# Block-sparse attention and a rational feed-forward: sampled key blocks copied by another engine, indices loaded four blocks at a time, factors in one instruction

## The chip, the cores and the metric

The kernel runs on one core of a Trainium2 chip. The metric is device time in microseconds, as the median of several runs. The engines are named as the profile names them: PE multiplies matrices (PEld loads its weights), DVE, ACT and POOL work on vectors, SP here only issues transfers (DMA). Each engine runs its instructions in the order in which the program was written for it.

## What is computed

Four batches of eight heads attend over 768 positions in 24 blocks of 32. A query block sees its neighbours, the first and the last block, and three sampled blocks; the first and last query block see all. The result, 3072 rows of 512, goes through a feed-forward whose activation is a quotient of polynomials.

```python
# attention: q, k, v are (4, 8, 768, 64)
scores = q @ k.T / sqrt(64)
mask = abs(blk_i - blk_j) <= 1
mask |= (blk_i == 0) | (blk_j == 0) | (blk_i == 23) | (blk_j == 23)
for qb in range(24):
    for kb in sampled_blocks[qb]:            # three per query block
        mask[qb*32:(qb+1)*32, kb*32:(kb+1)*32] = True
attn = softmax(where(mask, scores, -1e9))
x = (attn @ v) as (3072, 512)
# feed-forward: w_in is (512, 2048), w_out is (2048, 512)
h = x @ w_in
P = a[0] + a[1]*h + a[2]*h**2 + a[3]*h**3
Q = 1 + abs(b[0])*abs(h) + abs(b[1])*h**2
out = (P / (Q + 1e-6)) @ w_out
```

Weights and parameters `a`, `b` come as 64-bit floats, the indices as 64-bit integers; the kernel reads them as pairs of 32-bit words.

## The kernel before

**Tiles.** A key set (`kgs`, slices of the tile `kall`, and later `xkg`) holds eight blocks of keys: three neighbours, three sampled, the first and the last. A value set (`vgs`, shown as `vg`) holds the same eight blocks of values. The query block's scores against one key set are two tiles of 128 x 256 in `sp` (L903). DVE adds the bias of masked blocks and takes the maximum (`maxima`, L913), ACT takes the exponential (`exps`, L931), PE turns the result (L972), ACT evacuates it (`pT`, the helper's line L150), and PE multiplies it with the values (L1029, into `av`). Four query blocks together are weighted, turned and split into a high and a low half-precision part (`xh`, `xl`).

**Feed-forward.** Eight query blocks make a chunk of 256 rows; there are twelve chunks `c`. Each passes through eight units `u` of 256 columns of the hidden layer: 24 matmuls in (L1140 to L1142), the rational activation on ACT and DVE (L1147 to L1185), 12 matmuls out (L1196 to L1198). Each activation uses the factors in the tile `fc`, four per unit: the weight scale times 1, |b0|, a1 and a3. `factors` (L1114) writes them, for the first batch after each of four weight groups, for each later batch for all eight units at once.

**Weights.** The weights are decoded on the chip, one piece at a time: a transfer into `wl` (two buffers; L433 for `w_in`, L430 for `w_out`), a conversion (any of POOL, ACT, DVE, by the helper's line L150 or L154), three packing operations on DVE (L442, L445, L448), then scaling and splitting. This goes on while the first batch's attention and the first units run.

**The first batch's keys.** Its 24 key blocks stay in `kall`. Its sampled blocks are gathered from there: ACT copies three blocks of 128 x 256 in half precision into `kx` (two buffers, `kxs`; L856), each from an address in a register. Later batches gather keys by DMA from a scratch tensor `ks` (`kall<-ks`, L870 to L875). Values come by DMA in every batch (`vg`, L991 to L999): one transfer for the neighbours, two for the edges where they are not in place, three for the sampled blocks.

**The indices.** `ix` holds the clamped block numbers. `sampled_rows` (L795) loads the three of one query block into registers of the engine that needs them (TENSOR_LOAD): of SP for every query block and batch, of ACT for the first batch's copies. In a row of an order or a trace, ISA or FUSED_REGOPS beside a copy or a transfer is the arithmetic on such a register.

**The order.** Nothing is ordered by hand. Every piece of work is an `Op` with an engine (or several, by `among`), a price in nanoseconds, a priority and what it comes after. `issue` is a list scheduler: it simulates the engines with these prices and writes the program in the order in which its simulated engines take the pieces. A changed price or engine so changes the order on all engines. `fill` (L162) puts idle matmuls on PE where its simulation finds PE waiting in the first 80 us, to hold PE's clock.

Of the kernel before, what the change touches and what calls it, by code (L numbers as in the profile page):

```python
# [11 lines left out]
F32 = mybir.dt.float32  # L12
# [4 lines left out]
ALU = mybir.AluOpType  # L17
# [6 lines left out]
def kernel(  # L24
# [27 lines left out]
    nc = tc.nc  # L52
    B, H, S, D = q.shape
    DM, DFF = out.shape[1], w_out.shape[0]
    P = 128
    BLK = 32
    NB = S // BLK
    NR = sampled_blocks.shape[1]
# [15 lines left out]
    const = ctx.enter_context(tc.tile_pool(name="const", bufs=1))  # L74
# [21 lines left out]
    VE, SC, PO, TE, SY = "DVE", "Activation", "Pool", "PE", "SP"  # L96
# [193 lines left out]
    ix = const.tile([1, NB, 4], I32, name="ix")  # L290


    par = const.tile([P, 8], F32, name="par")
    absb = const.tile([P, 2], F32, name="absb")
    bias = const.tile([P, NB, NS], F32, name="bias")

    def load_small():
# [4 lines left out]
    def setup():  # L302
        nc.vector.tensor_scalar(out=ix[:, :, 0:NR], in0=samp[0:1].rearrange("p i (n w) -> p i n w", w=2)[:, :, :, 0],
                                scalar1=0, scalar2=NB - 1, op0=ALU.max, op1=ALU.min)
        nc.scalar.activation(out=absb, in_=par[:, 4:6], func=AF.Abs)

        sf = work[:, 2 * NR * NB:3 * NR * NB].rearrange("p (n i) -> p n i", n=NR)
        nc.vector.tensor_copy(out=sf, in_=samp.rearrange("p i (n w) -> p n i w", w=2)[:, :, :, 0])
        ii = work[:, 5 * NR * NB:5 * NR * NB + NB]
        nc.gpsimd.iota(ii, pattern=[[1, NB]], base=0, channel_multiplier=0, allow_small_or_imprecise_dtypes=True)  # L310
        dup = work[:, 3 * NR * NB:4 * NR * NB].rearrange("p (n i) -> p n i", n=NR)
        tmp = work[:, 4 * NR * NB:5 * NR * NB].rearrange("p (n i) -> p n i", n=NR)
        for r in range(NR):
            nc.vector.tensor_tensor(out=dup[:, r], in0=sf[:, r], in1=ii, op=ALU.subtract)
        nc.vector.tensor_tensor(out=dup, in0=dup, in1=dup, op=ALU.mult)
        nc.vector.tensor_scalar(out=dup, in0=dup, scalar1=1.0, scalar2=None, op0=ALU.is_le)
        for edge in (0.0, NB - 1.0):
            nc.vector.tensor_scalar(out=tmp, in0=sf, scalar1=edge, scalar2=None, op0=ALU.is_equal)
            nc.vector.tensor_tensor(out=dup, in0=dup, in1=tmp, op=ALU.max)
        for r in range(1, NR):  # L320
            for e in range(r):
                nc.vector.tensor_tensor(out=tmp[:, r], in0=sf[:, r], in1=sf[:, e], op=ALU.is_equal)
                nc.vector.tensor_tensor(out=dup[:, r], in0=dup[:, r], in1=tmp[:, r], op=ALU.max)
        nc.vector.memset(bias, 0.0)
        nc.vector.memset(bias[:, 1, 3 + NR:4 + NR], NEG)
        nc.vector.memset(bias[:, NB - 2, 4 + NR:5 + NR], NEG)
        for r in range(NR):
            nc.vector.tensor_scalar(out=bias[:, :, 3 + r], in0=dup[:, r], scalar1=NEG, scalar2=None, op0=ALU.mult)
# [195 lines left out]
    def block(j):  # L524
        return j + 1 if j < J else 0 if j == J else j
# [265 lines left out]

    def sampled_rows(x, eng=mybir.EngineType.SP):

        if (x, eng) not in rows_of:
            rows_of[x, eng] = nc.values_load_multi_w_load_instructions(  # L795
                ix[0:1, block(parts[x][1]), 0:NR], engines=[eng], min_val=0, max_val=NB - 1,
                skip_runtime_bounds_check_because="clamped when ix was written")[1]
        return rows_of[x, eng]

    def vrows(vg, kt, slot, n=1):  # L800
        return vg[slot * BLK:(slot + n) * BLK, kt].rearrange("p g a c -> p (g a c)")
# [21 lines left out]
    def attention(b, j, prio):  # L823
# [15 lines left out]
        for m, x in enumerate(xs):  # L839
            def one(m, x):  # L840
# [6 lines left out]
                if near and n > 1:  # L847
                    deps += [o for t in range(NCH) for o in k_evac[b, t]]
                    kslots = s_kall
                elif near:  # L850
                    s_kx = Slot(r_kx)

                    def copies():
                        rows = sampled_rows(x, mybir.EngineType.Activation)
                        for r in range(NR):
                            nc.scalar.copy(out=kxs[:, s_kx.buf, r].rearrange("p h r -> p (h r)"), in_=kall[:, bass.ds(rows[r], 1)].rearrange("p o h r -> p (o h r)"))  # L856

                    a = Op(SC, 1100, copies, [o_setup, chain["edges"]], p - 1, takes=[s_kx], uses=s_kall)
                    deps.append(a)
                    kslots = [s_kx] + s_kall  # L860
                else:
                    s_kg = Slot(r_kg)

                    def load():
                        kg, ks, = kgs[s_kg.buf], kv[b][0]
                        flat = kg.rearrange("p s h r -> p s (h r)")
                        if n > 1:
                            nc.sync.dma_start(out=flat, in_=ks[m * NS:(m + 1) * NS].rearrange("b p c -> p b c"))
                            return
                        nc.sync.dma_start(out=flat[:, 0:3], in_=ks[i - 1:i + 2].rearrange("b p c -> p b c"))  # L870
                        if h["new"]:
                            nc.sync.dma_start(out=flat[:, 3 + NR:], in_=ks[0:NB:NB - 1].rearrange("b p c -> p b c"))
                        rows = sampled_rows(x)
                        for r in range(NR):
                            nc.sync.dma_start(out=flat[:, 3 + r], in_=ks[bass.ds(rows[r], 1)].rearrange("o p c -> p (o c)"))  # L875

                    def price():
                        h["new"] = fresh("k", x, s_kg)
                        if n > 1:
                            return [(475, 524288)]  # L880
                        l = [(475, 196608)] + ([(475, 131072)] if h["new"] else [])
                        return l + [(860, 65536), (560, 65536), (560, 65536)]

                    a = Op(SY, price, load, [o_setup] + k_done[b], p - 1.95, takes=[s_kg], uses=[s_scr[b]], behind=chain.get("kg"))
                    chain["kg"] = a
                    deps.append(a)
                    kslots = [s_kg]
# [220 lines left out]
    def factors(b, u, n, after, prio):  # L1108

        def run():  # L1110
            if b not in fcs:
                fcs[b] = p2.tile([P, 4, NU], F32, name="fc")
            for j, coef in enumerate((1.0, absb[:, 0:1], par[:, 1:2], par[:, 3:4])):
                nc.vector.tensor_scalar(out=fcs[b][:, j, u:u + n], in0=wscale[:, u:u + n], scalar1=kv[b][3], scalar2=coef, op0=ALU.mult, op1=ALU.mult)  # L1114
        for x in range(u, u + n):
            o_fc[b, x] = None
        o = Op(VE, 700, run, after + [o_fc.get((b, 0))], prio)
        for x in range(u, u + n):
            o_fc[b, x] = o

# [246 lines left out]
```

## Time and profile before

| | |
|---|---|
| median of three timed runs | 882.49 us (882.07 to 882.88) |
| span of the profiled execution, first to last instruction | 879.5 us |
| its own time, taken as the median for want of another | 882.49 us, 3.0 around the span |
| busy PE / DVE / ACT / POOL | 824.0 / 730.5 / 676.5 / 111.5 us |
| granted clock of PE, mean | 0.985 |
| instructions on DVE / ACT / POOL | 1749 / 1449 / 115 |

The page also shows the span in 40 slices of 22 us; a digit is the busy share in tenths, 9 is 90% or more:

```
PE   8979686797899999899999999999999999999997
DVE  5658998999999888779878778878888787788886
ACT  6777897898678898987788768897898767588763
DMA  7797579868857955899556966899556966730000
```

Busy time on PE counts the filler too. Idle time of an engine that is not the bound costs nothing, so a stage is read by the engine that is full in it.

### The profile page before, as it was taken

How to read it: one execution, taken by the hardware profiler on the slowest of the kernel's cores; microseconds unless marked ns; L12 is line 12 of the kernel's file. 1: busy time of each engine (PE TensorE's matmuls, PEld its weight loads, DVE VectorE, ACT ScalarE, POOL GpSimd, SP SyncE). 2: the span in 40 equal slices, each digit the busy share in tenths (PEclk: the TensorE clock that was granted, in tenths of full speed). 3: DMA queues.
4: the chain of work that ended last, by engine and by line, in shares of the span. 5: the costliest groups of instructions: out<-in, count | busy, mean ns of one | idle time of the engine just before them, and what ended most of it. 6: DMA issues, size and time to landing. Idle time of an engine off the chain costs nothing.

```text
span 879.5 us, 27163 instructions
## 1 busy us (share of the span) xinstructions
PE 824.0 (94%) x10339; PEld 641.1 (73%) x10339; DVE 730.5 (83%) x1749; ACT 676.5 (77%) x1449; POOL 111.5 (13%) x115
## 2 busy tenths in 40 slices
PE   8979686797899999899999999999999999999997
PEld 4545465575678787778888787778788788788886
DVE  5658998999999888779878778888878787788886
ACT  6777897898678987788768887898767588767563
POOL 1123632616410000101000000100000000000000
PEclk9999899899999999999999999999999999999999
DMA  7797579868857955899556966899556966730000
GB/s 200 190 182 197 172 183 208 223 184 228 189 151 187 283 140 154 187 214 252 163 153 167 262 182 186 194 240 246 151 148 161 225 160 151 178 104 25 1 26 24
DMA packets 240209, 151.16 MB, mean 172 GB/s; under 512 B 16208, under 2 KB 222928, under 8 KB 240080
## 3 DMA queue, kind: packets, MB, share of 16 engines
q1 hardware_dynamic: 240080, 149.43, 68.6%
q8 instruction: 82, 1.34, 0.7%
q14 instruction: 47, 0.39, 0.2%
HBM read 132.07 MB, written 11.01 MB: 163 GB/s over the span
## 4 chain that ended last, share of the span: by engine, by line
PE 63%; DVE 13%; DMA 8%; SPq 7%; ACT 4%; issue 3%; POOL 1%; ACTq 0%; POOLq 0%; DVEq 0%
PE acc L1196 8%; PE ph L1140 8%; PE acc L1197 8%; PE acc L1198 8%; PE ph L1142 7%; PE ph L1141 7%; PE av L1029 5%; PE pt L972 4%; PE sp L903 4%; DMA vg<-in_v_dram 2%; SPq L999 2%; DMA wl<-in_moe_w_in_dram 2%; DVE pr L913 1%; DMA ldq<-in_q_dram 1%; DMA ld<-in_v_dram 1%
## 5 line engine op out<-in xcount | busy, mean ns | idle before, releaser
L1140 PE MATMUL ph<-xh,wi 128*128 128x256 f16 x768 | 211.7, 276 | 0.9 <-DVE tt L1157 0.9
L1141 PE MATMUL ph<-xl,wi 128*128 128x256 f16 x768 | 210.3, 274 | 0.0
L1142 PE MATMUL ph<-xh,wi 128*128 128x256 f16 x768 | 210.2, 274 | 0.0
L1196 PE MATMUL acc<-wo_h,gh 128*128 128x512 f32 x376 | 160.4, 427 | 0.2 <-ACT ld L150 0.2
L1198 PE MATMUL acc<-wo_h,gl 128*128 128x512 f32 x376 | 149.5, 398 | 3.8 <-DVE gl L1185 3.8
L1197 PE MATMUL acc<-wo_l,gh 128*128 128x512 f32 x376 | 149.1, 397 | 0.8 <-POOL wo_l L459 0.8
L1164 DVE SCALAR_TENSOR_TENSOR ab<-sq,absb,ab 128x512 f32<-128x512 f32 x96 | 73.3, 764 | 53.8 <-ACT ab L1161 53.8
L1147 ACT ACTIVATE sq<-ph,fc 128x512 f32<-128x512 f32 x96 | 65.7, 684 | 55.2 <-PE ph L1142 54.8
L1140 PEld LDWEIGHTS <-wi 128*128 128x128 f16 x768 | 75.4, 98 | 29.8 <-issue 16.2
L913 DVE CUSTOM_DVE_ANT_1 pr<-sp,bias 128x256 f32<-128x256 f32 x224 | 84.8, 418 | 8.3 <-PE sp L903 8.0
L931 ACT ACTIVATE pr<-pr,st,cqb 128x256 f32<-128x256 f32 x112 | 66.2, 594 | 31.0 <-DVE st L942 31.0
L1198 PEld LDWEIGHTS acc<-wo_h,gl 128*128 128x128 f32 x376 | 70.9, 189 | 21.6 <-DVE gl L1185 4.7
L1029 PE MATMUL av<-vg,pT 128*32 128x64 f32 x3584 | 74.9, 225 | 10.4 <-ACT pT L150 4.4
L1175 DVE SCALAR_TENSOR_TENSOR gh<-tt,par,rr 128x512 fp32r<-128x512 f32 x96 | 72.2, 752 | 14.4 <-PE acc L1197 12.9
L1196 PEld LDWEIGHTS acc<-wo_h,gh 128*128 128x128 f32 x376 | 71.3, 190 | 17.2 <-issue 2.1
L1029 PEld LDWEIGHTS av<-vg,pT 128*32 128x32 f32 x3584 | 56.9, 111 | 36.1 <-issue 14.6
L972 PE MATMUL pt<-ident,pr 128*128 128x128 f32 x448 | 74.6, 289 | 8.3 <-ACT pT L150 7.5
L1142 PEld LDWEIGHTS <-wi 128*128 128x128 f16 x768 | 75.5, 98 | 9.1
L972 PEld LDWEIGHTS pt<-ident,pr 128*128 128x128 f32 x448 | 68.0, 205 | 18.3 <-ACT pT L150 9.4
L1141 PEld LDWEIGHTS <-wi 128*128 128x128 f16 x768 | 75.6, 98 | 7.5
L1197 PEld LDWEIGHTS acc<-wo_l,gh 128*128 128x128 f32 x376 | 71.4, 190 | 13.0 <-POOL wo_l L459 1.7
L150 ACT ACTIVATE pT<-pt 128x512 f32<-128x512 f32 x112 | 66.3, 592 | 12.7 <-PE pt L972 12.0
(165 smaller groups left out, 1672.3 us busy)
## 6 DMA issues: line engine op xcount, KB each, us to landing
vg<-in_v_dram SPq DMA_DIRECT2D x312, 64.0 KB, 3.3
vg<-in_v_dram SPq DMA_DIRECT2D x88, 192.0 KB, 4.0
vg<-in_v_dram SPq DMA_DIRECT2D x24, 512.0 KB, 5.7
kall<-ks SPq DMA_DIRECT2D x49, 192.0 KB, 3.9
kall<-ks SPq DMA_DIRECT2D x147, 64.0 KB, 2.5
ld<-in_k_dram SPq DMA_DIRECT2D x36, 256.0 KB, 5.0
wl<-in_moe_w_in_dram SPq DMA_DIRECT2D x32, 256.0 KB, 4.4
wl<-in_moe_w_out_dram SPq DMA_DIRECT2D x16, 512.0 KB, 4.9
```

The costliest lines, as they stand in the source:

```text
L150: nc.scalar.activation(out=out, in_=in_, func=AF.Copy, scale=by)
L913: nc.vector.tensor_tensor_reduce(out=prs[x][:, g].rearrange("p (s r) -> p s r", r=BLK), in0=h["sp"][:, g].rearrange("p (s r) -> p s r", r= ...
L972: nc.tensor.transpose(pp[:, jj * P:(jj + 1) * P], cols, ident)
L1029: nc.tensor.matmul(av[rows, g], pT[:, 2 * g + kt, rows] if plain else pT[:, 2 * g + kt, pa_, rows], vf[:, g * HG + h4, kt * D:(kt + 1) * D ...
L1140: nc.tensor.matmul(o, wh, xh[:, :, cc], start=(cc == 0), stop=False)
L1141: nc.tensor.matmul(o, wh, xl[:, :, cc], start=False, stop=False)
L1142: nc.tensor.matmul(o, wl, xh[:, :, cc], start=False, stop=(cc == NCC - 1))
L1164: nc.vector.scalar_tensor_tensor(out=d["ab"], in0=d["sq"], scalar=absb[:, 1:2], in1=d["ab"], op0=ALU.mult, op1=ALU.add)
L1175: nc.vector.scalar_tensor_tensor(out=d["gh"], in0=d["tt"], scalar=par[:, 0:1], in1=d["rr"], op0=ALU.add, op1=ALU.mult)
L1196: nc.tensor.matmul(acc[:, t], ghs, wo_h[:, f], start=(new and e == 0), stop=False)
L1197: nc.tensor.matmul(acc[:, t], ghs, wo_l[:, f], start=False, stop=False)
L1198: nc.tensor.matmul(acc[:, t], gls, wo_h[:, f], start=False, stop=(last and e == 1))
```

## The change

Four edits, none of which changes what is computed:

- The copies of the first batch's sampled keys go from ACT to DVE, and their price for the scheduler from 1100 to 420 ns.
- `sampled_rows` loads the indices of four query blocks at once (three where an edge block is among them) and keeps the registers for the other three. SP's loads fall from 88 to 24; the copies' loads, 22 on ACT, become 6 on DVE.
- A weight group's four factors are one instruction over a tile `coef` of (1, |b0|, a1, a3), broadcast, in place of four; the price falls from 700 to 140.
- `setup` fills `coef` with four small DVE instructions.

```diff
+    coef = const.tile([P, 4], F32, name="coef")
...
         nc.scalar.activation(out=absb, in_=par[:, 4:6], func=AF.Abs)
+        nc.vector.memset(coef[:, 0:1], 1.0)
+        nc.vector.tensor_copy(out=coef[:, 1:2], in_=absb[:, 0:1])
+        nc.vector.tensor_copy(out=coef[:, 2:3], in_=par[:, 1:2])
+        nc.vector.tensor_copy(out=coef[:, 3:4], in_=par[:, 3:4])
...
-        if (x, eng) not in rows_of:
-            rows_of[x, eng] = nc.values_load_multi_w_load_instructions(
-                ix[0:1, block(parts[x][1]), 0:NR], engines=[eng], min_val=0, max_val=NB - 1,
+        b, j = parts[x][:2]
+        i = block(j)
+        if (b, i, eng) not in rows_of:
+            some = [n for n in (block(m) for m in range(j - j % 4, j - j % 4 + 4)) if n not in (0, NB - 1)]
+            values = nc.values_load_multi_w_load_instructions(
+                ix[0:1, some[0]:some[-1] + 1, 0:NR], engines=[eng], min_val=0, max_val=NB - 1,
                 skip_runtime_bounds_check_because="clamped when ix was written")[1]
-        return rows_of[x, eng]
+            for n, m in enumerate(some):
+                rows_of[b, m, eng] = values[n * NR:(n + 1) * NR]
+        return rows_of[b, i, eng]
...
-                        rows = sampled_rows(x, mybir.EngineType.Activation)
+                        rows = sampled_rows(x, mybir.EngineType.DVE)
                         for r in range(NR):
-                            nc.scalar.copy(out=kxs[:, s_kx.buf, r].rearrange("p h r -> p (h r)"), in_=kall[:, bass.ds(rows[r], 1)].rearrange("p o h r -> p (o h r)"))
+                            nc.vector.tensor_copy(out=kxs[:, s_kx.buf, r].rearrange("p h r -> p (h r)"), in_=kall[:, bass.ds(rows[r], 1)].rearrange("p o h r -> p (o h r)"))
-                    a = Op(SC, 1100, copies, [o_setup, chain["edges"]], p - 1, takes=[s_kx], uses=s_kall)
+                    a = Op(VE, 420, copies, [o_setup, chain["edges"]], p - 1, takes=[s_kx], uses=s_kall)
...
-            for j, coef in enumerate((1.0, absb[:, 0:1], par[:, 1:2], par[:, 3:4])):
-                nc.vector.tensor_scalar(out=fcs[b][:, j, u:u + n], in0=wscale[:, u:u + n], scalar1=kv[b][3], scalar2=coef, op0=ALU.mult, op1=ALU.mult)
+            nc.vector.scalar_tensor_tensor(out=fcs[b][:, :, u:u + n], in0=wscale[:, u:u + n].rearrange("p (o n) -> p o n", o=1).broadcast_to([P, 4, n]), scalar=kv[b][3],
+                                           in1=coef.rearrange("p (j o) -> p j o", o=1).broadcast_to([P, 4, n]), op0=ALU.mult, op1=ALU.mult)
-        o = Op(VE, 700, run, after + [o_fc.get((b, 0))], prio)
+        o = Op(VE, 140, run, after + [o_fc.get((b, 0))], prio)
```

The new prices change the scheduler's order on every engine. The number of fill matmuls falls from 201 to 182, and of the work that several engines may take, POOL has five operations fewer, DVE two fewer and ACT seven more.

The first place is DVE at the start of the first batch's attention, just ahead of the first maxima. `cq` and `hlq` belong to the queries, `kx` is the copies' target, `pr` the scores with their bias. Before:

```order
L741 SCALAR_TENSOR_TENSOR cq_451<-scq_425,sc0_236 128x1
L744 TENSOR_SCALAR cq_451<-cq_451 128x1
L747 TENSOR_SCALAR cq_451<-cq_451 128x1
L386 SCALAR_TENSOR_TENSOR hlq_453<-ldq_321,scq_425,hlq_453 128x8x64
L913 ISA pr_536,st_535<-sp_502,bias_102 128x256
L913 ISA st_535 128x1
```

After:

```order
L746 SCALAR_TENSOR_TENSOR cq_460<-scq_441,sc0_259 128x1
L803 TENSOR_LOAD ix_99
L866 ISA
L866 COPY kx_113<-kall_109 128x256
L866 ISA
L866 COPY kx_113<-kall_109 128x256
L866 ISA
L866 COPY kx_113<-kall_109 128x256
L391 SCALAR_TENSOR_TENSOR hlq_462<-ldq_344,scq_441,hlq_462 128x8x64
L749 TENSOR_SCALAR cq_460<-cq_460 128x1
```

A load of indices and three copies now stand on DVE between the queries' factors; two more sets of three follow before the first maxima. In all 39 copies and four loads stand ahead of the first unit's arithmetic, 27 copies and two loads behind.

The second place is SP between the third and the fourth piece of `w_in` (`wl`), with the value sets (`vg0` to `vg2`) between. Before:

```order
L433 DMA wl_734<-in_moe_w_in_dram 64x1024 x2
L993 DMA vg0_109<-in_v_dram 48x8x128
L795 TENSOR_LOAD ix_99
L999 ISA
L999 DMA vg0_109<-in_v_dram 16x8x128
L999 ISA
L999 DMA vg0_109<-in_v_dram 16x8x128
L999 ISA
L999 DMA vg0_109<-in_v_dram 16x8x128
L433 DMA wl_877<-in_moe_w_in_dram 64x1024 x2
```

After, from the last of the value sets that stand there:

```order
L1003 DMA vg1_111<-in_v_dram 48x8x128
L1009 ISA
L1009 DMA vg1_111<-in_v_dram 16x8x128
L1009 ISA
L1009 DMA vg1_111<-in_v_dram 16x8x128
L1009 ISA
L1009 DMA vg1_111<-in_v_dram 16x8x128
L438 DMA wl_1234<-in_moe_w_in_dram 64x1024 x2
L438 DMA wl_1255<-in_moe_w_in_dram 64x1024 x2
```

One value set stood between the third and the fourth piece, five stand there now, and the fifth piece follows at once; four of the five sets have no index load of their own.

## The prediction

> **What bounds the kernel now.** I read the table of stretches first, then the page's busy totals, then who waits for whom, then the chain. The columns of a stretch are its bounds, its length, and busy time (with the count) of PE, PEld, DVE, ACT and POOL, then granted clock, DMA share and GB/s.
>
> ```profile
> span 879.5 us, 27163 instructions
> 27.00:80.00 53.00, 46.02 (x719) 27.67 (x718) 32.99 (x102) 40.70 (x109) 13.33 (x16) 0.97 0.93 195
> 80.00:254.00 174.00, 140.57 (x2072) 105.29 (x2071) 170.12 (x409) 146.01 (x330) 74.63 (x64) 0.94 0.79 195
> 254.00:340.00 86.00, 86.00 (x1068) 69.41 (x1069) 77.25 (x204) 72.81 (x163) 2.85 (x3) 1.00 0.73 189
> 340.00:400.00 60.00, 56.09 (x758) 45.08 (x757) 45.10 (x115) 48.23 (x103) 3.54 (x4) 1.00 0.86 202
> 400.00:880.00 480.00, 471.43 (x5593) 382.11 (x5590) 388.71 (x863) 351.03 (x712) 12.85 (x16) 1.00 0.61 153
> L162 PE MATMUL acc<-ident 128*128 128x512 f16 x201 | 53.4, 402 | 1.7 <-DVE ident L93 1.7
> ```
>
> The filler alone (L162), a stretch before 100 us and the one behind, first PE and then PEld:
>
> ```profile
> 80.00:100.00 20.00, 6.41 (x25) 2.02 (x24) 0.89 0.49 148
> 100.00:120.00 20.00, 0.00 (x0) 0.00 (x0) 0.93 0.81 218
> ```
>
> Three stages. From 27 to 80 us no compute engine is full, DMA is (0.93), and much of what PE does is filler (53.4 us, none of it after 100 us). From 80 to 254 us DVE is busy 170.12 of 174 us and PE is not: DVE bounds it. From 254 us on PE is the bound: it stands idle 60 - 56.09 = 3.9 us from 340 to 400, and 8.6 us after. The span is therefore settled by how soon DVE gets through its work up to about 254 us, and by PE's few gaps behind. A microsecond taken off DVE between 80 and 254 us is a microsecond of the end; off ACT there (146 of 174) it is not.
>
> **The copies.** ACT's copies by stretch (its busy time), then their group, the price of an index load, and three rows that say how a load is hidden:
>
> ```profile
> 27.00:80.00 53.00, 9.77 (x30) 0.97 0.93 195
> 80.00:254.00 174.00, 12.05 (x36) 0.94 0.79 195
> L856 ACT COPY kx<-kall x66: 377/402/430, 26.9 to 176.4; 128x256 f16 x66
> L795 SPq TENSOR_LOAD <-ix x88: 664/675/1877, 13.9 to 754.9; - x88
> L795 ACTq TENSOR_LOAD <-ix x22: 696/703/932, 25.3 to 173.6; - x22
> 28.24 1.02 ACT L856 COPY kx<-kall 128x256 f16 x3 [0.36 <-issue]
> 35.04 1.00 ACT L856 COPY kx<-kall 128x256 f16 x3
> L442 DVE TENSOR_SCALAR dw<-dw x16: 411/416/1431, 85.7 to 240.6; 128x512 int32<-128x512 int32 x16
> L152 DVE COPY kall<-ph x6: 705/712/731, 18.1 to 26.1; 128x512 f16<-128x512 f16 x6
> ```
>
> Removed from ACT: 9.8 us before 80 us and 12.1 us after. The second part is off the path. The first sits in the attention's chain, but in a stretch whose DMA is full, so I book it at nothing; what is late next there is the transfer of values and weights.
>
> Added to DVE: 66 copies. No DVE copy of 128x256 f16 from SBUF is in the trace. Below: L442 moves four times the bytes in 0.41 us, a quarter is 0.10. Above: half of L152 (twice the elements, from PSUM), 0.36. I take 0.17, nearer to L442, which like the copy reads one operand in SBUF. In the new order 39 copies stand on DVE ahead of the first weight unit's arithmetic, which before began at 78.0 us (row below): 39 x 0.17 = 6.6 us, into the 53 - 32.99 = 20.0 us in which DVE idles from 27 to 80 us. Cost 0 while that cover lasts. What DVE waits for there is mainly the weights, not what the copies delay:
>
> ```profile
> DVE wi L442 <- POOL wi L154: 7.8, 4, 3.4
> DVE ab L1164 <- ACT ab L1161: 2.8, 1, 2.8
> 78.00 0.75 DVE L1164 SCALAR_TENSOR_TENSOR ab<-sq,absb,ab 128x512 f32<-128x512 f32 x1 [2.85 <-ACT ab L1161]
> ```
>
> The other 27 copies fall in the full stage: 27 x 0.17 = +4.6 us (2.7 to 9.7). They may also meet POOL, busy 74.63 of 174 us with operations of 74.63 / 64 = 1.2 us: nine groups of three, 0.43 of them met for half an operation, +2.3. Against this the new order gives POOL five operations fewer (conversions of weights go to ACT), 5.8 us; where two in five of them made DVE wait, that is as much. I let the two cancel.
>
> **The index loads.** 110 loads of three values become 30 of up to twelve, 24 on SP and 6 on DVE. A load stands ahead of each group of three copies: at 28.24 it left ACT idle for 0.36 of its 0.70 us, at 35.04 for none, since ACT had work queued. I take 0.35 us for one on DVE, four of them ahead of the first unit (in the idle 20 us, 0) and two in the full stage: +0.7. Below 0; above, if time goes by the values loaded, 4 x 0.70 = 2.8 us each.
>
> On SP 64 loads fewer are 64 x 0.675 = 43 us of its time, spread over all batches. Where SP sets the pace that is worth something. The chain of waits from 345 to 360 us runs through SP, where two of the longer pieces are index loads, and PE waits just then:
>
> ```profile
> 349.82 0.68 SPq L795
> 357.27 0.68 SPq L795
> 353.12 0.65 PE L1029 MATMUL av<-vg,pT 128*32 128x64 f32 x32 [0.90 <-DMA vg<-in_v_dram]
> 357.17 0.32 PE L343 MATMUL sp<-ident,mxq 128*128 128x128 f32 x1 [1.54 <-ACT scrap L392]
> ```
>
> Three of four loads gone at about 7 us apart over some 30 us is 2.0 us, and the two waits above are 2.4. A new order may open a gap elsewhere, 0.5: -1.5 us (-6 to +3).
>
> **The factors.** DVE's busy time in the three groups of four L1114 after 80 us; below, what one costs beside POOL and what it costs alone:
>
> ```profile
> 88.00:91.20 3.20, 3.11 (x4) 1.00 0.72 204
> 158.50:162.50 4.00, 3.98 (x4) 1.00 1.12 329
> 204.30:207.00 2.70, 2.62 (x4) 1.00 0.86 212
> 158.52 1.13 DVE L1114 TENSOR_SCALAR fc<-wscale,sc 128x2 f32<-128x2 f32 x1
> 159.56 1.20 DVE L1114 TENSOR_SCALAR fc<-wscale,sc,absb 128x2 f32<-128x2 f32 x1
> 158.46 3.39 POOL L506 TENSOR_TENSOR wi<-dw,wi 128x512 f16<-128x512 f32 x3
> 633.15 0.22 DVE L1114 TENSOR_SCALAR fc<-wscale,sc 128x8 f32<-128x8 f32 x1
> 633.28 0.28 DVE L1114 TENSOR_SCALAR fc<-wscale,sc,absb 128x8 f32<-128x8 f32 x1
> ```
>
> An instruction on two values takes 1.1 to 1.2 us while POOL works, 0.2 to 0.3 when it does not: it pays for waiting, once each. Twelve of them cost 9.7 us of the full stage. Three in their place, each 0.2 to 1.2, taken at 0.5: 1.5. Gain -8.2. The first group lies where DVE idles, and the later batches' groups lie under PE: 0. The four small instructions that fill coef stand ahead of a wait of DVE that ends on ACT at 12.34 us and was 3.98 us long:
>
> ```profile
> 12.34 0.16 DVE L613 TENSOR_REDUCE mx<-mx 128x1 f32<-128x6 f32 x1 [3.98 <-ACT scrap L392]
> ```
>
> Cost 0.
>
> **Sum.** Full stage +4.6 + 0.7 - 8.2 = -2.9; early stage 0; late stage -1.5: -4.4 on a span of 879.5, so 875.1. The timed median, 882.49, stands 3.0 above this span; I add it: 878.1 us. In the early stage bounds are -5 to +6: on the good side ACT's 9.8 us shorten attention by half, on the bad side the next rivals.
>
> **A rule against it.** All loads in the trace have three values, so 0.675 us may be a fixed price or 0.225 a value; no row can tell.
>
> The Trainium skill, "Runtime: NRT & Kernel Launch", section on instruction fetch mechanics, puts a register load at about 200 ns per register, in bulk too (for loads from HBM); by that page twelve values would be an estimated 2.4 us, DVE's six loads 14.4 us, and SP's saving nearly nothing. "DMA: Bandwidth & Descriptors", section on latency and other measured facts, gives instead a floor of about 600 ns for such a load, which would bear out the gain. The trace's 0.675 agrees with both, so I leave it a rival.
>
> **Rivals.** *A load goes by its values (slower).* Mechanism: DVE's in-order queue stands behind a load; maxima and weight packing wait, and PE for those. At 2.8 us, of which 0.7 is covered by queued work as at 35.04, each costs 2.1: two in the full stage 4.2 instead of 0.7, four early 8.4, half of it into the idle time, 4.2; SP's 1.5 is not gained. 878.1 + 3.5 + 4.2 + 1.5 = 887.3. It decides where two full and four half loads eat the 4.4 and their 0.7, from about 2.0 us a load. For it: the fit above. Against: loads were seen hidden.
>
> *The weights fall behind the values (no change).* SP issues the fourth piece of w_in one set of values after the third; in the new order five sets stand between. A set is
>
> ```profile
> vg<-in_v_dram SPq DMA_DIRECT2D x312, 64.0 KB, 3.3
> vg<-in_v_dram SPq DMA_DIRECT2D x88, 192.0 KB, 4.0
> ```
>
> 192 + 3 x 64 = 384 KB, four more are 1.5 MB, at 195 GB/s 7.9 us. If the first unit starts that much later and attention done in the meantime returns only half, +4: 882.1. Against: five sets stand there because attention runs earlier.
>
> *Attention gains too (more).* DVE's idle 20 us shrinks by 6 as scores stop waiting for ACT: 872.
>
> **How the numbers follow.** Forecast 0.42, more gain 0.12, no change 0.22, slower 0.24. What this kernel's measurement can tell from no change is 0.2%, 1.8 us. Faster 0.54, same 0.22, slower 0.24. The range leaves out the best and worst tenths: 870 to 889; the forecast's own is 874 to 880.7.
>
> **What would show it.** By the changed file's lines: right are L866 at 0.1 to 0.25 us on DVE, L803 near 0.7 us on both queues, L1123 below 0.6 us; DVE still full from 80 to 250 us; PE without gaps some 3 us sooner; less than 3.9 us idle about 340 to 400. Wrong: L803 of 2 us or more with DVE idle behind it, copies of 0.35 us or more, or the first L1150 over 5 us later with no attention ahead to show for it; then the sum is off by its place.

## The result, and the profile after

The changed kernel is slower: 890.56 us in the median of six runs (888.86 to 895.68) against 881.92 of the kernel before beside it, a ratio of 1.0109 with a 95% interval of 1.0085 to 1.0133. The forecast was 878.1 us. The profiled execution of after has a span of 888.2 us.

The stretches of after, with the columns as before:

```profile
span 888.2 us, 27041 instructions
27.00:80.00 53.00, 44.98 (x796) 26.00 (x795) 33.62 (x153) 31.03 (x80) 9.25 (x13) 0.94 0.84 186
80.00:254.00 174.00, 137.49 (x1866) 103.85 (x1866) 160.36 (x394) 133.43 (x286) 72.09 (x62) 0.87 0.75 192
254.00:340.00 86.00, 84.84 (x1029) 68.30 (x1027) 73.86 (x178) 71.91 (x160) 2.92 (x3) 0.98 0.76 207
340.00:400.00 60.00, 58.68 (x764) 47.15 (x762) 51.67 (x139) 49.09 (x103) 6.33 (x7) 1.00 0.70 188
400.00:880.00 480.00, 476.45 (x5722) 386.33 (x5720) 392.91 (x870) 356.21 (x724) 13.10 (x15) 1.00 0.58 152
400.00:860.00 460.00, 456.45 (x5603) 369.90 (x5601) 375.12 (x844) 346.61 (x709) 13.10 (x15) 1.00 0.60 159
```

The last stretch of before, up to 860 us too:

```profile
400.00:860.00 460.00, 456.45 (x5517) 370.32 (x5515) 376.15 (x845) 345.62 (x704) 12.85 (x16) 1.00 0.63 159
```

The loss is in the first 254 us. DVE, which had 3.9 us to spare between 80 and 254 us, now has 13.6 (174 - 160.36), although it was given more to do. PE's granted clock there falls from 0.94 to 0.87. Behind it PE is a little fuller than before only from 340 to 400 us, where it is idle for 1.3 us (3.9 before). From 400 to 860 us it is idle for 3.55 us in both kernels. The rows to 880 us can't be compared: before ends at 879.5 us, so its thinly filled last microseconds all lie in the row, while after runs on to 888.2.

Followed through the trace, the output matmuls of unit 24 (counted from 0, in the order of execution) begin at 346.0 us before and at 358.9 after, 12.9 us later; those of unit 88 at 841.8 and 850.6, 8.8 later. So some 13 us are lost early and 4 are gained back by unit 88.

The three parts by their groups, of after. (Two of DVE's six loads and eight of SP's 24 carry nine values, because an edge block is among their four; the others carry twelve.) A group's row has the shortest, median and longest duration in ns, then its first and last start:

```profile
L803 SPq TENSOR_LOAD <-ix x24: 1908/2528/2724, 13.9 to 751.0; - x24
L803 DVEq TENSOR_LOAD <-ix x6: 2115/2828/3067, 27.4 to 168.6; - x6
L866 DVEq FUSED_REGOPS  x66: 57/57/65, 30.5 to 181.3; - x66
L866 DVE COPY kx<-kall x66: 173/220/1302, 30.6 to 183.3; 128x256 f16 x66
L1123 DVE SCALAR_TENSOR_TENSOR fc<-wscale,sc,coef x7: 247/391/1112, 75.5 to 642.1; 128x8 f32<-128x8 f32 x4, 128x32 f32<-128x32 f32 x3
```

Copies and factors have medians of 0.22 and 0.39 us, near the forecast's 0.17 and 0.5; some of each take over 1 us. A load of twelve values takes 2.53 us on SP and 2.83 on DVE; one of three took 0.675 and, on ACT, 0.70. It goes by its values.

For whom DVE waits from 27 to 80 us, in after (us in total, times, longest):

```profile
DVE kx L866 <- issue: 7.0, 3, 3.1
DVE xn L1073 <- PE av L1039: 5.1, 1, 5.1
DVE kx L866 <- PE sp L913: 4.0, 3, 2.6
DVE xl L1097 <- ACT xh L150: 1.6, 1, 1.6
```

The first row is the load itself: no engine releases the copy, and a load of 2.79 us on DVE, begun at 71.56, ends just ahead of the copy at 74.53. The second is new in kind: the weighing of query blocks 4 to 7 (`xn`) waits for value matmuls, and it stands in DVE's row ahead of the packing of the fourth piece of `w_in`. The steps to the first unit, in the trace of before and then of after:

```profile
52.37 0.69 DVE L445 SCALAR_TENSOR_TENSOR wi<-wl,wi 128x512 int32<-128x512 int32 x1
62.57 0.22 DVE L489 COPY wscale<-scw 128x1 f32<-128x1 f32 x2
62.58 2.06 POOL L154 TENSOR_SCALAR dw<-wi,scw 128x512 f32<-128x512 f32 x3 [10.71 <-DVE scw L360]
65.30 0.69 DVE L1063 TENSOR_TENSOR xn<-av,sm 128x512 f32<-128x512 f32 x1 [1.14 <-PE av L1029]
73.88 0.27 PE L1140 MATMUL ph<-xh,wi 128*128 128x256 f16 x1
```

```profile
61.71 0.69 DVE L1073 TENSOR_TENSOR xn<-av,sm 128x512 f32<-128x512 f32 x1 [5.06 <-PE av L1039]
64.31 0.66 POOL L154 TENSOR_SCALAR wi<-wl 128x512 f32<-128x512 f32 x1 [14.54 <-DMA wl<-in_moe_w_in_dram]
65.46 0.69 DVE L450 SCALAR_TENSOR_TENSOR wi<-wl,wi 128x512 int32<-128x512 int32 x1
74.53 0.50 DVE L866 COPY kx<-kall 128x256 f16 x3 [2.83 <-issue]
75.19 2.03 POOL L154 TENSOR_SCALAR dw<-wi,scw 128x512 f32<-128x512 f32 x3 [10.22 <-DVE scw L365]
84.32 0.28 PE L1150 MATMUL ph<-xh,wi 128*128 128x256 f16 x1
```

Before, the fourth piece is packed at 52 us, the scale is ready at 62.6 and the weighing comes after that. After, the weighing comes first and waits, the fourth piece comes from memory only at 64.3, and a load of twelve values (2.83 us) stands in the middle of the scale's small steps. POOL gets the scale 12.6 us later, the first unit begins 10.4 us later.

### The profile page after: what moved, and what is told of

Same layout as the page of the kernel before. It is cut to its first block, busy times and chain, and to the rows that moved or that the text cites. A ratio compares the mean times of both kernels' runs of the same rounds, so it can differ in the third digit from the quotient of the medians.

```text
span 888.2 us, 27041 instructions
## 1 busy us (share of the span) xinstructions
PE 828.8 (93%) x10320; PEld 645.5 (73%) x10320; DVE 731.1 (82%) x1796; ACT 659.8 (74%) x1390; POOL 108.0 (12%) x110
## 4 chain that ended last, share of the span: by engine, by line
PE 61%; DVE 16%; ACT 7%; SPq 6%; DMA 5%; issue 4%; DVEq 1%; POOL 0%; POOLq 0%; ACTq 0%
PE ph L1150 8%; PE acc L1206 8%; PE acc L1208 7%; PE acc L1207 7%; PE ph L1151 7%; PE ph L1152 7%; PE av L1039 5%; PE sp L913 4%; PE pt L982 4%; SPq L1009 2%; ACT pr L941 2%; DVE pr L923 2%; DMA wl<-in_moe_w_in_dram 1%; DVE gh L1185 1%; DMA ldq<-in_q_dram 1%
## 5 line engine op out<-in xcount | busy, mean ns | idle before, releaser
L1150 PE MATMUL ph<-xh,wi 128*128 128x256 f16 x768 | 214.5, 279 | 2.0 <-DVE tt L1167 2.0
L1151 PE MATMUL ph<-xl,wi 128*128 128x256 f16 x768 | 212.9, 277 | 0.0
L1152 PE MATMUL ph<-xh,wi 128*128 128x256 f16 x768 | 212.8, 277 | 0.0
L1174 DVE SCALAR_TENSOR_TENSOR ab<-sq,absb,ab 128x512 f32<-128x512 f32 x96 | 72.5, 755 | 58.5 <-ACT ab L1171 58.4
L1150 PEld LDWEIGHTS <-wi 128*128 128x128 f16 x768 | 76.6, 100 | 30.2 <-issue 16.6
L982 PE MATMUL pt<-ident,pr 128*128 128x128 f32 x448 | 76.9, 292 | 12.2 <-ACT pT L150 7.3
L1185 DVE SCALAR_TENSOR_TENSOR gh<-tt,par,rr 128x512 fp32r<-128x512 f32 x96 | 74.7, 778 | 16.0 <-PE acc L1207 12.6
L1151 PEld LDWEIGHTS <-wi 128*128 128x128 f16 x768 | 76.6, 100 | 10.5 <-issue 2.0
L1152 PEld LDWEIGHTS <-wi 128*128 128x128 f16 x768 | 76.5, 100 | 10.2
L1207 PEld LDWEIGHTS acc<-wo_l,gh 128*128 128x128 f32 x376 | 71.7, 191 | 12.6 <-POOL wo_l L464 0.8
L941 ACT ACTIVATE pr<-pr,st,cq 128x256 f32<-128x256 f32 x112 | 66.2, 597 | 19.0 <-DVE st L952 19.0
```

The lines of the kernel that those rows point to most:

```text
L941: nc.scalar.activation(out=prs[x][:, g], in_=prs[x][:, g], func=AF.Exp, scale=Q["first"]["c"], bias=st[:, 6 + g:7 + g], accum_out=total if ...
L982: nc.tensor.transpose(pp[:, jj * P:(jj + 1) * P], cols, ident)
L1150: nc.tensor.matmul(o, wh, xh[:, :, cc], start=(cc == 0), stop=False)
L1151: nc.tensor.matmul(o, wh, xl[:, :, cc], start=False, stop=False)
L1152: nc.tensor.matmul(o, wl, xh[:, :, cc], start=False, stop=(cc == NCC - 1))
L1174: nc.vector.scalar_tensor_tensor(out=d["ab"], in0=d["sq"], scalar=absb[:, 1:2], in1=d["ab"], op0=ALU.mult, op1=ALU.add)
```

## The experiments

"The planner" is the list scheduler. Each kernel was timed in five rounds against the kernel before on the same chip; the median is followed by the ratio to it with its 95% interval.

### One part after another, in two orders

**Factors alone.** The kernel before, with the one instruction for a group's factors. The price of 700 is kept, so the planner writes the same order; the four small instructions that fill `coef` come with it.

```diff
-            for j, coef in enumerate((1.0, absb[:, 0:1], par[:, 1:2], par[:, 3:4])):
-                nc.vector.tensor_scalar(out=fcs[b][:, j, u:u + n], ...)
+            nc.vector.scalar_tensor_tensor(out=fcs[b][:, :, u:u + n], ...)
         o = Op(VE, 700, run, ...)
```

> The kernel before with the factors in one instruction alone, at the old price, so that the order stays. My prediction's term (each of the twelve instructions beside POOL paid a wait of its own): 8 us less, 873 to 876. Rival (the wait for POOL moves to the next instruction that needs it): 2 to 3 us less, 879 to 881.

875.75 us, 0.9926 (0.9898 to 0.9954): -6.5 us. The term of the factors, -8.2, is nearly there, and the rival's 2 to 3 us lie outside the interval. The seven instructions take 3.7 us in all, 525 ns each:

```profile
L1118 DVE SCALAR_TENSOR_TENSOR fc<-wscale,sc,coef 128x8 f32<-128x8 f32 (+1 forms) x7 | 3.7, 525 | 0.0
```

**Copies in the old order.** The kernel before, the copies and their loads of three values issued on DVE, at the places where ACT's stood in the plan:

```diff
-                        rows = sampled_rows(x, mybir.EngineType.Activation)
+                        rows = sampled_rows(x, mybir.EngineType.DVE)
-                            nc.scalar.copy(out=kxs[...], ...)
+                            nc.vector.tensor_copy(out=kxs[...], ...)
                     a = Op(SC, 1100, copies, ...)
```

> The kernel before, its order kept (the scheduler still plans the copies on ACT at 1100 ns), with the copies issued on DVE and loads of three. Theory A: copies cost little, 27 to 36 of them at 0.17 us in DVE's full stage, +3 to +6 us, ACT's relief early takes half back: 882 to 886. Theory B (only the new order is bad): no change or a gain, 878 to 882.

887.47 us, 1.0057 (1.0037 to 1.0078): +5.0 us. Its copies between 80 and 254 us (busy time of DVE, count, clock, DMA share, GB/s):

```profile
80.00:254.00 174.00, 7.39 (x36) 0.89 0.79 188
```

DVE is as full from 80 to 254 us as before (170.17 us busy, 170.12 before) although copies are 7.39 us of it, so some 7 us of its other work come later. The time lies above both expectations. The loss is of the size of what the copies take of a full DVE; what ACT's relief gives back was not measured apart.

**Factors and copies in the old order.** Both of these edits.

> The old order with both: copies issued on DVE (loads of three) and factors in one instruction. Against the changed kernel with loads of three (888.0) only the order differs. If the two edits add (+0.57% and -0.74%): 880 to 882. Theory B then puts 6 to 7 us on the new order. Theory C: 886 to 888, the same as in the new order.

883.15 us, 1.0014 (0.9996 to 1.0032). Against the factors alone the copies cost 0.88%, 7.8 us. The gain of one part is spent by the other. In both of these kernels the copies stand where the order planned them for ACT; the third order below has them at places planned for DVE.

**Grouped loads in the old order.** The kernel before with `sampled_rows` of after; six loads of up to twelve values on ACT, 24 on SP.

> The kernel before with the grouped loads alone (24 of twelve values on SP, 6 on ACT), order kept. Theory A (by value): SP's sum of loads stays near 60 us, ACT waits about 2 us in each of its six, early ones on the path: +2 to +6 us, 884 to 888, and no gain from SP late. Rival (a fixed price, the long loads of the changed kernel come from elsewhere): -2 us, 879 to 880.

882.40 us, 0.9981 (0.9958 to 1.0004): nothing that the measurement can tell. The rows say why:

```profile
L798 SPq TENSOR_LOAD <-ix x24: 1903/2526/2716, 13.8 to 743.7; - x24
L798 ACTq TENSOR_LOAD <-ix x6: 1981/2653/2828, 25.2 to 141.8; - x6
```

16 loads of twelve values and 8 of nine are 16 x 2.53 + 8 x 1.91 = 55.8 us on SP, and 88 x 0.675 = 59.4 before: there was next to nothing to save.

**After with loads of three.** The kernel after with `sampled_rows` of before; order, copies and factors as in after.

> The changed kernel with one edit taken back: indices are loaded three at a time again (88 loads on SP, 22 on DVE), order and copies stay. Theory A (a load goes by its values: 2.83 us for twelve, DVE idle 11.1 us before the copies): loads fall back to about 0.68 us, DVE's idle time before the copies to under 3 us, the kernel wins 6 to 9 us back, to 880 to 884. Theory B (the new order itself is late: the first unit starts at 84 instead of 74 us, PE's granted clock sinks to 0.87 between 80 and 254 us): idle time goes, but time stays at 886 to 890.

887.96 us, 1.0055 (1.0034 to 1.0077). So twelve values a load cost 0.54% on DVE. And this kernel does the same work as the one with factors and copies in the old order (1.0014), apart from 182 filler matmuls in place of 201 and some conversions that went from POOL and DVE to ACT: the new order costs 0.41%, with intervals that only just don't overlap. The profiled execution of this run is its longest, 6.6 us above the median, and some 2.6 us late before any of this begins (its first matmuls into `ph` start at 18.3 us, in after at 15.7). Its times within the trace are to be read with that in mind.

**Loads of six**, after with two blocks to a load.

> The kernel after with its order, and loads of six values (two blocks) in place of twelve. A load goes by its values: 1.4 us each on VectorE and 1.35 us on SP (3 values took 0.75 and 0.67, 12 took 2.83 and 2.53), 44 of them on SP, and the ratio between that with loads of three (1.0055) and that with twelve (1.0109), near 1.007. Rival (the load's floor counts, values cost little, and twelve are slow for another reason): below 1.0 us each, ratio 1.005 or less.

884.14 us, 1.0036 (1.0018 to 1.0055). The durations follow the values, the ratio doesn't lie between its neighbours as expected. Twelve values are worse than three or six; between these two the intervals overlap.

```profile
L803 SPq TENSOR_LOAD <-ix x48: 664/1298/2692, 13.8 to 757.4; - x48
L803 DVEq TENSOR_LOAD <-ix x12: 743/1429/1814, 27.3 to 176.3; - x12
```

**The new order with the copies on ACT.** After with loads of three, the copies issued on ACT at DVE's places.

> The changed kernel's order kept (the scheduler still plans the copies on DVE at 420 ns), but the copies are issued on ACT, with loads of three; factors in one instruction. Its counterpart in the old order is the run with factors alone (875.8). Theory B (the new order itself is late): 882 to 886, so 6 to 10 us over its counterpart, although DVE carries no copies. Theory C (the copies' 0.16 to 0.2 us each on a full DVE explain the loss, order costs nothing): 875 to 879.

888.85 us, 1.0070 (1.0046 to 1.0095), the same as with the copies on DVE (1.0055). Taking the copies off DVE gains nothing here, although DVE is busy for only 154.19 us from 80 to 254. That doesn't show that the copies cost nothing on DVE: they now stand in ACT's row at places planned for DVE, and in the third order (below) that alone loses time.

### Which order, and why

**A third order.** After with loads of three; the planner is told a price of 700 for the copies, and nothing else is changed.

```diff
-                    a = Op(VE, 420, copies, ...)
+                    a = Op(VE, 700, copies, ...)
```

> The changed kernel with loads of three, the copies priced at 700 instead of 420 ns for the scheduler: a third order of the same instructions, in which three sets of values instead of five stand between the weights' third and fourth piece. Theory B in the form that the weights fall behind the values: the first unit starts some 5 us earlier than at 84 to 86 us and the time falls to 881 to 885. If it is not the weights, time stays within 2 us of 888.

876.16 us, 0.9950 (0.9928 to 0.9972), against 1.0055 for the same work at a price of 420 (DVE, ACT and POOL have as many instructions in both, PE has four filler matmuls more). The order alone is worth 1.05%, 9.3 us. Only one set of values, not three as expected, stands on SP between the third and the fourth piece, as in the kernel before; the fourth is issued at 49.2 us, in after at 58.5. The first unit begins at 68.6 us. Waits of DVE from 27 to 80 us:

```profile
DVE kx L861 <- issue: 5.1, 8, 1.0
DVE xl L1092 <- ACT xh L150: 1.5, 1, 1.5
```

The wait for value matmuls is gone.

**Factors with their new price.** The kernel before with the one instruction at 140 in place of 700, so that the planner writes another order, with the copies still on ACT.

> The kernel before with factors in one instruction, priced at 140 ns, so that the scheduler orders anew; copies stay on ACT, weights and values alternate as before. If a new order is harmful as such: 878 to 882. If only the order that puts values ahead of weights is harmful: 873 to 877, like factors alone in the old order (875.8).

877.09 us, 0.9944 (0.9924 to 0.9965). A smaller price does not by itself make a bad order.

**The weights' loads moved.** The row of SP in after puts the fourth piece of `w_in` behind five sets of values. Here it is e1_loads_of_three with two loads moved up, and no other row of any engine changed:

```diff
+                if b == 0 and j in {4: 3, 7: 4}:           # set of block j: piece
+                    ol.first = [loaded[{4: 3, 7: 4}[j]]]   # issued ahead of it
...
+            for z in o.first:
+                z.run()
+                z.ran = True
```

> The kernel after with loads of three values, as in the run e1_loads_of_three (ratio 1.0055), every engine's row word for word as there but SP's: two loads of w_in are moved forward in SP's queue, the fourth piece past three sets of values and the fifth past one. Theory (the new order costs because the fourth piece stands behind the values): the fourth piece is issued near 45 us in place of near 58, the first unit's matmuls begin at least 4 us sooner than in e1_loads_of_three, VectorE is fuller from 80 to 254 us (over 165 us busy in place of 163.8), and the ratio falls to 0.996 to 1.002. Rival (the order on VectorE and ScalarE costs, with attention's work ahead of the packing of weights; where the load stands is nothing, as the packing stands behind attention anyway): the first unit within 2 us of e1_loads_of_three, ratio 1.0035 to 1.0075.

892.66 us, 1.0122 (1.0085 to 1.0158): worse, by 0.67% of e1_loads_of_three, and above the rival's range too. The theory fell. In the trace the fourth piece is issued at 44.8 us, past four sets of values. The first unit begins at 86.0 us, as it did (86.2). DVE and PE of this run:

```profile
DVE xn L1078 <- PE av L1042: 9.7, 1, 9.7
```

```profile
63.42 1.08 PE L1042 MATMUL av<-vg,pT 128*32 128x64 f32 x32 [3.96 <-DMA vg<-in_v_dram]
```

The weights are there sooner, but DVE doesn't reach them: it stands at the weighing, whose values are now the late ones, for 9.7 us in place of 5.6.

**The weighing moved too.** So the weighing must go back behind the scale, with the value matmuls of block 7 that it waits for. In the first try:

```diff
+            if o.held:            # values of block 7, weighing, turning, xh, xl
+                late.append((o, e))
...
+            if o.until:           # the first group's factors
+                for z, y in late:
+                    z.run(...)
```

> e14_weights_moved (ratio 1.0122) with one group moved back besides: the value matmuls of the block 7, the weighing of the blocks 4 to 7 that waits for them, and its turning and storing come behind the first weight group's factors, in the rows of TensorE, VectorE and ScalarE, as in the kernel before; all other instructions stand as in e14_weights_moved. Theory (on VectorE and TensorE the packing of the fourth piece and the scales of the first weight group stand behind a weighing that waits for values; each row is worked off in its order, so a load that comes sooner gains nothing until this group is moved too): the packing of the fourth piece ends before 62 us in place of about 71, the first unit begins before 79 us in place of 86.0, ratio 0.998 to 1.005. Rival (VectorE owes the same work by 254 us in whatever order, and the new order's loss has many small places): the first unit at 82 us or later, or sooner with a ratio that stays at 1.008 or above.

898.77 us, 1.0198 (1.0175 to 1.0221). In this kernel the matmuls of block 7 come behind the load of block 10's values into the same buffer, so they multiply with block 10's values in place of block 7's (the kernel no longer computes the attention), and wait for them:

```profile
PE av L1047 <- DMA vg<-in_v_dram: 11.1, 3, 9.8
```

That wait is the edit's own; the run doesn't test the theory. The second try lets that load come behind them as well:

> e14_weights_moved (ratio 1.0122) with one group moved back besides, as in e15_weigh_moved: value matmuls of the block 7, the weighing of the blocks 4 to 7, its turning and storing come behind the first weight group's factors; and the load of the values of block 10, which shares a buffer with block 7 and in e15_weigh_moved came ahead of the matmuls of block 7, so that they waited for it to 79 us, comes behind them. Theory (the scales of the first weight group stand behind a weighing that waits for values, on VectorE and TensorE): the fourth piece is packed before 60 us in place of 71, the factors near 69 us, the weighing right behind them, the first unit begins between 76 and 80 us in place of 86.0, ratio 0.999 to 1.006. Rival (the loss has many small places, and the first unit's start is only its sign): a first unit before 81 us with a ratio of 1.008 or above.

886.41 us, 1.0057 (1.0031 to 1.0084): 0.65% better than with the loads moved alone, and its interval lies below that one. The ratio is as the theory has it, the first unit isn't: 82.8 us, where 76 to 80 were expected. DVE of this run:

```profile
55.56 0.69 DVE L465 SCALAR_TENSOR_TENSOR wi<-wl,wi 128x512 int32<-128x512 int32 x1
62.22 0.43 DVE L459 TENSOR_SCALAR wi<-wi 128x512 int32<-128x512 int32 x1 [5.96 <-ACT wi L151]
70.74 0.39 DVE L1138 SCALAR_TENSOR_TENSOR fc<-wscale,sc,coef 128x8 f32<-128x8 f32 x1
71.05 0.68 DVE L1085 TENSOR_TENSOR xn<-av,sm 128x512 f32<-128x512 f32 x1
```

The fourth piece is packed by 56.3 us, and the weighing waits for nothing. But now the packing of the fifth piece, next in the row and ahead of the scale's steps, waits 5.96 us for its conversion, which waits for its transfer. One wait is taken out and the next one in the row takes part of its place. The move is thereby shown to matter against the loads moved alone. Both moves together gain nothing against e1_loads_of_three (1.0055), where neither was made, and the first unit's times can't decide more: after, e1_loads_of_three and loads of six have one and the same order on DVE, ACT, POOL and PE up to 120 us, and in their profiled executions it begins at 84.3, 86.2 and 79.8 us. That this one place carries the loss of the new order is not shown.

**The planner told to interleave.** After with loads of three and its prices; the sets of values of blocks 2, 4 and 6 stand behind the fourth, fifth and sixth piece, and the planner plans all engines around that. Further lines make the planner wait for a piece in `also`.

```diff
+                if b == 0 and j in {2: 3, 4: 4, 6: 5}:
+                    ol.also = [loaded[{2: 3, 4: 4, 6: 5}[j]]]   # order only
```

> The kernel after with loads of three values and prices as they are (copies 420, factors 140), but the planner is told that the values of the blocks 2, 4 and 6 stand behind the fourth, fifth and sixth piece of w_in on SP; it then plans all engines anew. Theory (weights behind values cost): the first unit's matmuls begin before 76 us, VectorE is full again from 80 to 254 us (over 168 us busy), ratio 0.992 to 1.000. Rival (the small prices themselves spoil the plan, as the planner thinks that VectorE has room that it hasn't): ratio 1.002 to 1.008.

882.32 us, 1.0008 (0.9986 to 1.0030), just above the theory's range and below the rival's, and 0.47% better than e1_loads_of_three. The first unit begins at 77.7 us, and DVE is busy for 168.59 of 174 us. So a plan with weights and values interleaved gets back about what the new order had cost; as all engines were planned anew, it doesn't say by which of its places.

Kernels with the copies on DVE in orders planned for that (in two of them pieces were then moved by hand), by how much of DVE is used from 27 to 254 us. Busy time and first unit are of one profiled execution each, which lay up to 6.6 us from its kernel's median:

| kernel | DVE busy, us | first unit, us | ratio |
|---|---|---|---|
| after (twelve values) | 194.0 | 84.3 | 1.0109 |
| weights' loads moved | 196.6 | 86.0 | 1.0122 |
| after with loads of three | 198.5 | 86.2 | 1.0055 |
| weighing moved too | 198.8 | 82.8 | 1.0057 |
| loads of six | 201.5 | 79.8 | 1.0036 |
| interleaved | 205.8 | 77.7 | 1.0008 |
| third order | 210.6 | 68.6 | 0.9950 |

From after to the third order DVE is busy for 16.6 us more by 254 us, and the ratio falls by 1.59%, 14.0 us. The two ends agree nearly one for one; the rows between don't (the second has 2.6 us more than the first and isn't faster), so the table shows that the two go together, no more.

### Versions beyond both

**Third order, copies on ACT.** e10_third_order with the copies issued on ACT.

> e10_third_order (ratio 0.995), every engine in the same order, with the copies and their loads issued on ScalarE again; the factors stay one instruction. If a copy on VectorE costs what it did in the old order (0.9926 without and 1.0014 with, a difference of 0.0088): 0.984 to 0.989. If VectorE has room in this order: 0.993 to 0.997.

884.67 us, 1.0032 (1.0013 to 1.0051): 0.82% slower than with the copies on DVE, where a gain or no change had been expected. Its DVE doesn't get ahead without the copies; from 27 to 80 us it waits for PE and ACT:

```profile
DVE xn L1068 <- PE av L1034: 4.6, 1, 4.6
DVE pr L918 <- PE sp L908: 4.4, 5, 1.2
DVE xl L1092 <- ACT xh L150: 2.8, 2, 1.5
```

Here an order planned for one engine is a bad order with the work on another. That ACT has no gaps where the copies need them is how I read these waits; it was not tried.

**Factors and grouped loads, old order, copies on ACT.**

> The kernel before, in its order, with the factors in one instruction (0.9926 alone) and the indices loaded for four blocks at a time (0.9981 alone), the copies left on ScalarE. If the two act apart: 0.989 to 0.993. If the grouped loads, whose twelve values on ScalarE take 2.65 us each, now come to lie on the path because the units start sooner: 0.994 to 0.998.

878.39 us, 0.9968 (0.9951 to 0.9985): grouping seems to spoil a part of the factors' gain (0.9926), but the two intervals overlap a little. No kernel is better than the one with the factors alone: 875.75 us, faster than before and than after. The third order (0.9950) and the factors replanned (0.9944) can't be told from it.

## Why the prediction was wrong

Four kernels lead from before to after, each with one thing more; their ratios give the terms (882 us to 1, and each step is known to some 0.3%, 2.6 us). The terms belong to this path: in the third order copies on DVE with loads of three stand at 0.9950 against 0.9926 for the factors alone, a difference within the noise, where the table's second and third step are 11.4 us together.

| step | from, to | measured | forecast |
|---|---|---|---|
| factors | 1, 0.9926 | -6.5 us | -8.2 |
| copies on DVE | 0.9926, 1.0014 | +7.8 | +4.6 |
| new order | 1.0014, 1.0055 | +3.6 | 0 early, -1.5 late |
| twelve values a load | 1.0055, 1.0109 | +4.8 | +0.7 |
| sum | 1, 1.0109 | +9.6 | -4.4 |

- *What bounds the kernel.* Right: DVE up to 254 us, and a microsecond there is one at the end. It was read as a property of the kernel, though; it belongs to the order. In the new order DVE is not full (160.36 of 174 us), and what it waits for counts.
- *Factors.* Right in mechanism and nearly in size: what each small instruction paid is saved by having fewer of them, and that wait did not simply move to the next instruction.
- *Copies.* The price of 0.17 us was good early: 5.86 us for the 36 copies before 80 us in after, 0.16 each (with 57 ns for a register operation beside each). In the full stage the term was too small: 9.29 us for 30 copies, 0.31 each, against 4.6. All seven copies of over 0.3 us lie beside an operation of POOL, and meeting POOL was the +2.3 that was let cancel. In the old order the copies cost 0.57% to 0.88%, 5.0 to 7.8 us, within the bounds of 2.7 to 9.7 us.
- *Early stage at nothing.* This step failed. The 20 idle microseconds were counted as cover for copies and loads, but idle time in an engine that works in order is no store to be drawn on: it lies at certain waits. The new waits (7.0 us of issue, 5.1 for the weighing) are added at other places, ahead of the first unit. In after DVE's idle time from 27 to 80 us is still 53 - 33.62 = 19.4 us. Its busy time there grew by 0.63 us only, with 5.86 us of copies in it, so 5.2 us of other work are missing there: about 1 us is saved by the factors' first group, and some 4 were pushed behind 80 us, into the full stage.
- *Loads.* The step "0.35 us for one on DVE" failed, and the saving of 43 us on SP with it. Durations of 0.675, 1.298 and 2.528 us for 3, 6 and 12 values on SP make 0.21 us a value; on DVE 0.748, 1.429 and 2.828, 0.23 a value. In place of 43 us SP saved 59.4 - 55.8 = 3.6 by the medians, over the whole run. The Trainium skill, "Runtime: NRT & Kernel Launch", section on instruction fetch mechanics, puts a register load at about 200 ns per register, in bulk too (for loads from HBM); the trace agrees for these loads from SBUF (2.53 us for twelve).
- *Late stage.* The term of -1.5 for SP's relief failed, as there was next to none. The 8.6 us of idle after 400 us were misread as well: up to 860 us PE idles 3.55 us, and the rest is the end of the kernel, where little is left to multiply. The lag does shrink by 4.1 us from unit 24 to unit 88. PE's idle time between those two points falls from 7.5 us (495.84 - 488.38) to 4.9 (491.72 - 486.86), and PE has 1.5 us less work there. With loads of three the lag also falls, from 16.1 to 13.4 us, so it isn't the long loads. Why the later units catch up was not settled:

```profile
346.00:841.84 495.84, 488.38 (x6073) 395.59 (x6071) 400.65 (x923) 377.60 (x774) 16.39 (x20) 1.00 0.68 169
358.89:850.61 491.72, 486.86 (x6042) 394.68 (x6039) 402.00 (x920) 374.59 (x769) 18.74 (x21) 1.00 0.63 166
```

- *The rivals.* "A load goes by its values" named the right mechanism, 4.8 us against its estimate of 9.2 over the forecast. "The weights fall behind the values" had the right place and the right signal: a first unit later by 10.4 us where 7.9 were worked out. It counted on attention to give half of that back; attention was ahead when the first unit began (352 value matmuls were done, 256 in the kernel before), but at unit 24 the lag was 12.9 us. And it had only the place on SP as the cause, which moving the two loads alone (1.0122) didn't bear out. Each was given alone, and both came together.

## What to carry to other kernels

When a change alters a price in a list scheduler, cost the new order as a part of its own: look in each in-order row for what now stands ahead of the work that starts the next stage, and for what that waits. Time in which an engine idles hid added work here only at the wait where it lay. And before several small loads are made one, find whether the price is by the load or by the value; a trace with one size can't say.

## What the runs showed of the hardware

- A register load from SBUF takes time by its values: about 0.23 us a value on DVE and 0.21 on SP, from three to twelve, with next to no fixed part. What stands behind it in the engine's queue waits for all of it (idle of 2.83 us ahead of a copy at 74.53 us).
- PE's granted clock differs between kernels, and the time doesn't follow it. From 80 to 254 us its mean is 0.94 before, 0.87 in after and 0.87 in the third order, whose units start earliest and which is faster than before. From 100 to 120 us it is 0.66 in after and 0.93 before. Over its whole executions the kernel before ranged from 0.974 to 0.987. How much of the loss the clock is, no run separates. After from 100 to 120 us, then the third order:

```profile
100.00:120.00 20.00, 14.09 (x179) 10.65 (x170) 20.00 (x51) 11.98 (x22) 13.36 (x12) 0.66 0.71 180
80.00:254.00 174.00, 142.02 (x1930) 108.42 (x1928) 170.14 (x429) 137.10 (x294) 71.86 (x60) 0.87 0.81 197
```

- A DVE copy of 128x256 half-precision elements within SBUF, from an address in a register, has a median of 220 ns in after; on ACT it took 402 before. Beside an operation of POOL it took up to 1.30 us.
